# Attention in one kernel with an MLP: the output row tile of the preceding chunk in place of one step's weighted sums

## The chip, the cores and the metric

The kernel runs on one core of a Trainium2 chip. The metric is the device time of one execution in microseconds (us). Five engines work from queues of their own, each in program order: PE (TensorE: matmuls; its weight loads are shown as PEld), ACT (ScalarE), DVE (VectorE), POOL (GpSimd) and SP (SyncE, which here only issues DMAs). They wait for one another through semaphores.

## The reference

All of it is float32; x is 1 x 2048 x 448, there are 16 heads of 28 columns, and k and v have one head that all 16 query heads share.

```python
xn = _layernorm(x)
q = (xn @ wq).reshape(B, S, H, Dh).transpose(0, 2, 1, 3)     # H = 16, Dh = 28
k, v = xn @ wk, xn @ wv
p = softmax(einsum("bhqd,bkd->bhqk", q, k) * Dh ** -0.5)
o = einsum("bhqk,bkd->bhqd", p, v)                           # weighted sums
A = o.transpose(0, 2, 1, 3).reshape(B, S, H * Dh) @ wo       # output projection
y = _layernorm(xn)
Bm = gelu(y @ w1 + b1) @ w2 + b2                             # F = 1792
out = x + A + Bm
```

## The kernel before

The program has three stages: normalisation and the q, k, v projections; the MLP, whose result plus x is kept in DRAM (`ad`); and attention, which ends with the output projection. The instructions of each engine stand in the order in which the Python code emits them (a manual schedule), so the order of the loops is the order on every queue.

Attention works on 16 *units* `u`, numbered from 0. A unit is a chunk `c = u // 4` of 512 query rows and a group `g = u % 4` of four heads. A unit goes through 16 key tiles `kt` of 128 keys, in eight *steps* `i` = 0 to 7; `n = 8u + i` counts steps over all units. In each step the string ORDER says in which order kinds of work are emitted:

- `s`: a score, L694: one matmul of 128 keys by 512 queries for one head `j` into a PSUM tile `m`, and its exponential on ACT into a tile `p` (L695). SHARES gives eight or seven of these per step. `p` tiles come in 12 pairs (PAIRS), 24 in all.
- `M` and `X`, `Y`: preparation for the following units. `M` is a matmul for the score maxima (L523), whose transpose and reduce run on DVE (L530, L531); there is one in each of steps 3 to 6, in which only seven scores are done. `X` and `Y` shift, exponentiate (L538 on ACT) and transpose back (L544) the scores of the next unit's first key tile.
- `n`: one stage of the normalisation of the preceding unit's sums (L807 to L822), which ends in the pair `oth`, `otl` (the high and low part of the normalised sums, pool tiles with 5 buffers each, kept in `ots[c, g]`).
- `P`: the weighted sums, L880. BURST = 2 key tiles are taken from the queue `pvq`, each with four matmuls of 128 x 32 weights that write four bands of one PSUM tile `po`. In the trace each of them has two records. The queue runs behind the scores: step i of a unit sums key tiles 2i-2 and 2i-1, step 0 the last two of the unit before.
- `o`: one stage of the stream `oside`. When a chunk's fourth unit is summed, `o_wait` first loads four row tiles from `ad` over eight steps, and then `o_jobs` emits one *output row tile* per step through `o_part`: 12 matmuls of 128 x 128 weights and 448 columns (three for each of the four groups, L767 to L769) into one PSUM tile `m`, an add on DVE (L772) and a store (L773). The four row tiles of chunk 0 so fall into unit 5, those of chunk 1 into unit 9, those of chunk 2 into unit 13, in steps 1 to 4, between that step's scores. The row tiles of chunk 3 are done after the last unit (`end_jobs`), except a first part in the last step.

PSUM tiles `m` come from seven buffers in turn (`mtile`: four in `rings`, three in `mp`), for scores, maxima and row tiles alike: a matmul that starts a tile waits until the seventh tile before it has been read.

`load_rows_of` takes a tile `a` (four buffers), writes one element of it on DVE (L755) so that the load has something to wait on, and loads the row tile on SP's queue (L756).

Of the kernel before, what the change touches and what calls it, by code (L numbers as in the profile page):

```python
# [9 lines left out]
F32R = mybir.dt.float32r  # L10
# [5 lines left out]
P = 128  # L16
S, D, H, DH, F = 2048, 448, 16, 28, 1792
NT = S // P
CT = 4
NCH = NT // CT  # L20
CW = CT * P
NG = H // 4
# [3 lines left out]
BURST = 2  # L26
# [14 lines left out]
def block_kernel(ctx, tc, x, wq, wk, wv, wo, w1, b1, w2, b2, out):  # L41
# [4 lines left out]
    def f(t):  # L46
        return t.bitcast(F32)
# [62 lines left out]
    def mtile(shape):  # L110
        if rings:
            given.append(0)
            if len(given) % 7 > 3 or len(given) % 7 == 0:
                return rings[0].tile(shape, F32, name="m")
        return mp.tile(shape, F32, name="m")
# [94 lines left out]
    def bn_end(c, k0=0, n=CT):  # L210
        for k in range(k0, k0 + n):
            dve.bn_aggr(lnp[:, CT * c + k, :], sts[c][:, k, :])
        ts = slice(CT * c + k0, CT * c + k0 + n)
        r = rstd(lnr[:, ts], lnp[:, ts, 1], n)
        next(r)
        yield
        next(r)
        dve.scalar_tensor_tensor(lnb[:, ts], lnp[:, ts, 0], -1.0, lnr[:, ts], op0=ALU.mult, op1=ALU.mult)
        yield
# [9 lines left out]
    def norm_both():  # L229
        dve.tensor_mul(lnq, lnp[:, :, 1], lnr)  # L230
        dve.tensor_mul(lnq, lnq, lnr)
        r = rstd(lnq, lnq, NT)
        next(r)
        yield
        next(r)
        yield
        turned = mtile([NT, P])
        pe.transpose(turned, lnq, ident)
        rows = wp.tile([NT, P], F32, name="rows")
        dve.tensor_copy(rows, turned)  # L240
        nc.scalar.dma_start(second, rows)
        act.activation(warm, one, AF.Tanh)
        yield
# [162 lines left out]
    for c, at in ((2, ((0, 1), (0, 2), (0, 2), (0, 3))), (3, ((1, 0), (1, 1), (1, 2), (1, 3)))):  # L406
        for k in range(CT):
            later(*at[k], lambda t=CT * c + k: bn(t))
        g = bn_end(c)
        for k in range(2):  # L410
            later(c - 1, 0, lambda g=g: next(g), True)
    g = norm_both()
# [11 lines left out]
    units = [(c, g) for c in range(NCH) for g in range(NG)]  # L424
    NU = len(units)
    qss, ots = {}, {}
# [3 lines left out]
    for c in range(NCH):  # L430
        if c + 1 < NCH:
            center, turn = norm_parts(c + 1)
        for i in range(4):
# [17 lines left out]
            if (c, i) in w1_turns:  # L451
                n = w1_turns.index((c, i))
# [117 lines left out]
                    self.gens.pop(0)  # L570
            return False

    side, oside = Stream(), Stream()

    ph1b = ExitStack()
    hp = ph1b.enter_context(tc.tile_pool(name="hp", bufs=1))
# [124 lines left out]
    for n in range(len(mslots) + LAG):  # L701
        c, ft = mslots[n] if n < len(mslots) else (NCH, n - len(mslots))
# [29 lines left out]
    att = ctx.enter_context(tc.tile_pool(name="att", bufs=2))  # L732
# [19 lines left out]
    def load_rows_of(c, tiles):  # L752
        for k in tiles:
            rows[c, k] = keep.tile([P, D], F32, name="a", bufs=4)
            dve.memset(rows[c, k][0:1, 0:1], 0.0)  # L755
            nc.sync.dma_start(rows[c, k], ad[:, CT * c + k, :])  # L756
# [3 lines left out]
    def o_part(c, k, gs):  # L760
        if gs[0] == 0:
            parts[c, k] = mtile([P, D])
        po = parts[c, k]
        ts = slice(k * P, (k + 1) * P)
        for g in gs:
            oth, otl = ots[c, g]
            pe.matmul(po, oth[:, ts], woh[:, g, :], start=(g == 0), stop=False)  # L767
            pe.matmul(po, oth[:, ts], wol[:, g, :], start=False, stop=False)  # L768
            pe.matmul(po, otl[:, ts], woh[:, g, :], start=False, stop=(g == NG - 1))  # L769
        if gs[-1] == NG - 1:  # L770
            a = rows[c, k]
            dve.tensor_add(a, a, parts.pop((c, k)))  # L772
            (nc.scalar if k % 2 and c == NCH - 1 else nc.sync).dma_start(ov[:, CT * c + k, :], a)  # L773

    def o_jobs(c):
        for k in range(CT):
            o_part(c, k, range(NG))
            yield

    def o_tiles(c, g):  # L780
        ots[c, g] = [att.tile([P, CW], F32R, name=n, bufs=5) for n in ("oth", "otl")]
        return ots[c, g]

    def watch(u, sums):
# [5 lines left out]
    def judge_sum():  # L790
        whole = att.tile([P, 1], F32, name="whole", bufs=1)
        dve.tensor_reduce(whole, seen, axis=AX.X, op=ALU.add)
        return whole
# [29 lines left out]
        yield  # L823

    def end_jobs(u, po, halves_of):
        while side.step() or oside.step():
            pass
        c, g = units[u]
        oth, otl = o_tiles(c, g)
        tr, rb, on = att.tile([P, CW], F32, name="tr2", bufs=1), att.tile([P, CW], F32, name="tr", bufs=1), att.tile([P, CW], F32, name="oc", bufs=1)  # L830
        rc = att.tile([P, CW // 32], F32, name="rc", bufs=1)
        halves_of(1)
        sq = att.tile([P, CW], F32, name="sq", bufs=1)
        act.activation(sq, po, AF.Square, accum_out=seen[:, u:u + 1])
        for k in (1, 2):
            o_part(c, k, range(NG - 1))

        def blocks(t, h):
            return t[:, h].rearrange("p (a b) -> p a b", b=32)

        def shares(i):
            h, r = slice(256 * i, 256 * i + 256), slice(8 * i, 8 * i + 8)
            dve.transpose(tr[:, h], po[:, h])
            dve.reciprocal(rc[:, r], blocks(tr, h)[:, :, 0])
            dve.transpose(blocks(rb, h), rc[:, r, None].to_broadcast([P, 8, 32]))
            dve.tensor_mul(on[:, h], po[:, h], rb[:, h])
            act.activation(oth[:, h], on[:, h], AF.Copy)
            return lambda: dve.tensor_sub(otl[:, h], on[:, h], f(oth[:, h]))

        shares(0)()  # L850
        whole = judge_sum()
        low = shares(1)
        o_part(c, 0, [g])
        o_part(c, 1, [g])
        low()
        o_part(c, 3, range(NG - 1))
        judge(whole)
        o_part(c, 2, [g])
        o_part(c, 3, [g])
# [15 lines left out]
    def pv(u, kt):  # L875
        if kt == 0:
            pos[u] = op.tile([P, CW], F32, name="po")
        po = pos[u]
        for j in range(4):
            pe.matmul(po[32 * j:32 * j + 32, :], vs[:, kt, :], ps.pop((u, kt, j)),  # L880
                      start=(kt == 0), stop=(kt == NT - 1))
        if kt == NT - 1:
            side.add(norm_jobs(u, pos.pop(u)))
            side.step()
            c, g = units[u]
            if c < NCH - 1 and g == NG - 1:
                oside.add(o_wait(c))

    def o_wait(c):
        for k in range(CT):  # L890
            load_rows_of(c, [k])
            yield
            yield
        yield from o_jobs(c)

    xside = Stream()
    pvq = [(u, kt) for u in range(NU) for kt in range(NT)]
    last = NU * NT // 2 - 1
    for u in range(NU):
        todo = [(u, kt, j) for kt in range(1 if u else 2, NT) for j in range(4)]  # L900
        for i in range(NT // 2):
            n = NT // 2 * u + i
            if n == last - 13:
                load_rows_of(NCH - 1, range(CT))
            if n == 9:
                load_wo()
            if 12 <= n < 12 + NG:
                prep_wo(n - 12)
            if i == 0 and u + 2 < NU:
                load_q(u + 2)  # L910
            jobs = todo[:SHARES[i] if u else 8 * (i > 0)]
            todo = todo[len(jobs):]
            maxima = [(u + 2, i - 3 - (u == 0))] if 3 + (u == 0) <= i < 7 + (u == 0) else []
            if u == 0 and i in (1, 2):
                maxima = [(1, 2 * i - 2), (1, 2 * i - 1)]
            for what in ORDER:
                if what == "s" and jobs:
                    score(*jobs.pop(0))
                elif what == "M":
                    for v, j in maxima:  # L920
                        if v < NU:
                            max_job(v, j)
                elif what in "XY":
                    if what == "X" and i == (2 if u else 3) and u + 1 < NU:
                        xside.add(shift_jobs(u + 1))
                    xside.step()
                elif what == "e":
                    if i == 7 and u + 2 < NU:
                        load_max(u + 2)
                    if n == 2:  # L930
                        load_max(1)
                elif what == "n":
                    side.step()
                elif what == "o":
                    if n == last:
                        o_part(NCH - 1, 0, range(NG - 1))
                    oside.step()
                elif what == "P":
                    assert not jobs
                    for _ in range(BURST if n else 0):  # L940
                        pv(*pvq.pop(0))
        assert not todo
    assert pvq and all(u == NU - 1 for u, kt in pvq)
    pv_last(NU - 1, [kt for u, kt in pvq])
    while side.step():
        pass
    while oside.step():
        pass

    def full_max(u):  # L950
# [79 lines left out]
```

## Time and profile before

| | |
|---|---|
| median of 3 runs | 897.25 us (896.04 to 898.35) |
| the profiled execution | 897.27 us |
| its span, first to last instruction | 895.2 us |
| mean granted TensorE clock | 0.998 |

The attention stage fills a little more than the second half of the span: the first copy of L807, which ends unit 0, starts at 382.4 us, and the last one at 851.3 us. The profile's numbers are us from the start of the span, unless marked ns. In the rows of a timeline the first number is the start, the second how long the group of merged instructions lasted, and what stands in square brackets is the engine's idle time ahead of the group and what ended it.

### The profile page before, as it was taken

To read this page: it belongs to the slowest core of one execution; us is meant where nothing else is said; L and a number is where in the kernel's file an instruction comes from. 1 tells how busy PE (TensorE), PEld (TensorE's weight loads), DVE (VectorE), ACT (ScalarE), POOL (GpSimd) and SP (SyncE) were. 2 spreads that over 40 slices of the span, in tenths; PEclk is the share of its full clock that TensorE was granted. 3 is DMA by queue.
4 is the path that set the end of the run, shared out by engine and by line. 5 is a ranking of instruction groups with operands and counts; after the bars stand their busy time and mean duration, and the time that the engine had idled before them with its cause. 6 is when DMAs were issued, how large, how long until landed. Compare 5 with 4: busy or idle time off the path is not lost.

```text
span 895.2 us, 13235 instructions
## 1 busy us (share of the span) xinstructions
PE 883.6 (99%) x4914; PEld 563.6 (63%) x4914; DVE 485.4 (54%) x963; ACT 703.7 (79%) x1334; POOL 72.8 (8%) x82
## 2 busy tenths in 40 slices
PE   9999999999999999999999999999999999999997
PEld 8777888888888886444444564444564444564445
DVE  6757766656556767555464544464544564544212
ACT  5767564545454467999999979999969999969993
POOL 5450000000000002040000000000000000000000
PEclk9999999999999999999999999999999999999999
DMA  9975232023003004031102201102211102211001
GB/s 303 316 233 191 82 127 83 1 77 112 1 3 111 2 11 124 2 78 43 43 1 63 74 31 43 34 10 63 63 42 43 32 12 63 64 41 43 1 1 44
DMA packets 36297, 60.69 MB, mean 68 GB/s; under 512 B 7782, under 2 KB 23348, under 8 KB 35204
## 3 DMA queue, kind: packets, MB, share of 16 engines
q1 hardware_dynamic: 34644, 58.95, 21.7%
q10 hardware_dynamic: 1584, 0.84, 0.4%
q8 instruction: 40, 0.66, 0.3%
q14 instruction: 29, 0.24, 0.1%
HBM read 39.89 MB, written 18.88 MB: 66 GB/s over the span
## 4 chain that ended last, share of the span: by engine, by line
PE 86%; ACT 5%; DVE 4%; DMA 3%; issue 1%; SPq 0%; POOL 0%; ACTq 0%; DVEq 0%; POOLq 0%
PE m L694 27%; PE po L880 25%; PE ph L178 11%; PE m L630 4%; PE m L633 4%; PE m L627 4%; ACT p L695 2%; PE m L523 2%; PE m L767 1%; PE m L768 1%; PE m L769 1%; PE ph L181 1%; PE ph L183 1%; DMA qd<-qe 1%; PE qp L178 1%
## 5 line engine op out<-in xcount | busy, mean ns | idle before, releaser
L695 ACT ACTIVATE p<-m 128x512 f32<-128x512 f32 x956 | 491.2, 771 | 29.8 <-PE m L694 29.4
L694 PE MATMUL m<-xh,ks 128*128 128x512 f32 x960 | 272.7, 410 | 0.7 <-DVE tt L530 0.3
L694 PEld LDWEIGHTS m<-xh,ks 128*128 128x128 f32 x960 | 174.3, 188 | 149.4 <-ACT p L695 76.3
L880 PE MATMUL po<-p,vs 128*32 128x512 f32 x2016 | 242.4, 598 | 0.0
L880 PEld LDWEIGHTS po<-p,vs 128*32 128x32 f32 x2016 | 52.6, 109 | 115.9 <-issue 115.9
L600 ACT ACTIVATE hz<-hx,b1s 128x512 f32<-128x512 f32 x56 | 40.6, 724 | 101.8 <-DVE hx L597 101.8
L530 DVE STREAM_TRANSPOSE tt<-m 128x512 f32<-128x512 f32 x60 | 43.0, 716 | 111.3 <-PE m L523 111.3
L633 PE MATMUL m<-w2h,hl 128*128 128x448 f32 x224 | 81.9, 366 | 0.1
L627 PE MATMUL m<-w2h,hh 128*128 128x448 f32 x224 | 81.9, 366 | 0.0
L630 PE MATMUL m<-w2l,hh 128*128 128x448 f32 x224 | 81.9, 365 | 0.0
L604 DVE SCALAR_TENSOR_TENSOR hz<-hz,hx 128x512 f32<-128x512 f32 x56 | 38.8, 692 | 52.0 <-ACT hx L601 52.0
L807 DVE COPY oc<-po 128x512 f32<-128x512 f32 x15 | 10.4, 692 | 103.2 <-PE po L880 103.2
L178 PE MATMUL ph<-xh,w1h 128*128 128x512 f32 x159 | 63.1, 397 | 2.0 <-DVE hx L597 2.0
L178 PE MATMUL ph<-xh,w1l 128*128 128x512 f32 x159 | 62.3, 392 | 0.0
L178 PE MATMUL ph<-xl,w1h 128*128 128x512 f32 x159 | 62.3, 392 | 0.0
L822 POOL TENSOR_TENSOR otl<-oc,oth 128x512 fp32r<-128x512 f32 x15 | 23.9, 1591 | 470.2 <-DVE oth L820 244.5
L597 DVE TENSOR_TENSOR hx<-ph,xn 128x512 f32<-128x512 f32 x53 | 36.4, 687 | 39.8 <-PE ph L183 39.6
L538 ACT ACTIVATE tt<-tt 128x512 f32<-128x512 f32 x60 | 51.4, 857 | 0.0
L544 DVE STREAM_TRANSPOSE p<-tt 128x512 f32<-128x512 f32 x60 | 42.1, 702 | 12.0 <-ACT tt L538 12.0
L627 PEld LDWEIGHTS m<-w2h,hh 128*128 128x128 f32 x224 | 42.1, 188 | 5.4 <-issue 0.4
L630 PEld LDWEIGHTS m<-w2l,hh 128*128 128x128 f32 x224 | 42.1, 188 | 4.5
L633 PEld LDWEIGHTS m<-w2h,hl 128*128 128x128 f32 x224 | 42.1, 188 | 4.1 <-DVE hl L615 0.7
(173 smaller groups left out, 1032.2 us busy)
## 6 DMA issues: line engine op xcount, KB each, us to landing
xh<-qd SPq DMA_DIRECT2D x64, 224.0 KB
qd<-qe SPq DMA_DIRECT2D x24, 256.0 KB
a<-in_A_x_dram SPq DMA_DIRECT2D x20, 224.0 KB
ad<-a SPq DMA_DIRECT2D x16, 224.0 KB
a<-ad SPq DMA_DIRECT2D x16, 224.0 KB
raw<-in_B_w_dram SPq DMA_DIRECT2D x7, 448.0 KB
out_dram<-a SPq DMA_DIRECT2D x14, 224.0 KB
xd<-xh SPq DMA_DIRECT2D x2, 1024.0 KB
```

Of the source, the lines that this page charges most:

```text
L178: pe.matmul(ps, w, v, start=(n == 0), stop=False)
L530: dve.transpose(tts[u, j], pm)
L538: act.activation(tts[u, j], tts[u, j], AF.Exp, scale=SCALE)
L544: dve.transpose(p0s[u][:, j], tts.pop((u, j)))
L600: act.activation(hz, hx, AF.Square, bias=b1s[:, ft:ft + 1], scale=GELU[0] ** 0.5)
L604: dve.scalar_tensor_tensor(hz, hz, 1.0, hx, op0=ALU.add, op1=ALU.mult)
L627: pe.matmul(m2[k], hh[:, ts], w2h, start=(ft == 0), stop=False)
L630: pe.matmul(m2[k], hh[:, ts], w2l, start=False, stop=False)
L633: pe.matmul(m2[k], hl[:, ts], w2h, start=False, stop=(ft == NF - 1))
L694: pe.matmul(s, ks[:, kt * P:(kt + 1) * P], qss[u][:, j, :], start=True, stop=True)
L695: act.activation(p, s, AF.Exp, scale=SCALE)
L880: pe.matmul(po[32 * j:32 * j + 32, :], vs[:, kt, :], ps.pop((u, kt, j)), start=(kt == 0), stop=(kt == NT - 1))
```

## The change

Row tiles of chunks 0 to 2 are no longer a stream of their own. Each unit from 4 on does one of them: unit u does row tile u % 4 of chunk u // 4 - 1, in step 5, at the place `P` where that step's two key tiles would be summed. These two are summed in step 6 with step 6's own, four key tiles in a row. The row tile's row is loaded at the start of the unit; the rows of the last chunk are loaded in the last two steps. `oth` and `otl` get 8 buffers each, since a chunk's pairs are now kept until the next chunk's last unit. `oside`, `o_wait` and its calls go.

```diff
     def o_tiles(c, g):
-        ots[c, g] = [att.tile([P, CW], F32R, name=n, bufs=5) for n in ("oth", "otl")]
+        ots[c, g] = [att.tile([P, CW], F32R, name=n, bufs=8) for n in ("oth", "otl")]
...
         if kt == NT - 1:
             side.add(norm_jobs(u, pos.pop(u)))
             side.step()
-            c, g = units[u]
-            if c < NCH - 1 and g == NG - 1:
-                oside.add(o_wait(c))
-
-    def o_wait(c):
-        for k in range(CT):
-            load_rows_of(c, [k])
-            yield
-            yield
-        yield from o_jobs(c)
...
+    o_steps = {(u, 5): (u // NG - 1, u % NG) for u in range(NG, NU)}
...
-            if n == last - 13:
-                load_rows_of(NCH - 1, range(CT))
+            if n >= last - 1:
+                load_rows_of(NCH - 1, (range(CT - 1), [CT - 1])[n - last + 1])
+            for v, step in o_steps:
+                if v == u and i == 0:
+                    load_rows_of(o_steps[v, step][0], [o_steps[v, step][1]])
...
                 elif what == "o":
                     if n == last:
                         o_part(NCH - 1, 0, range(NG - 1))
-                    oside.step()
                 elif what == "P":
                     assert not jobs
-                    for _ in range(BURST if n else 0):
+                    if (u, i) in o_steps:
+                        o_part(*o_steps[u, i], range(NG))
+                        continue
+                    for _ in range((BURST if n else 0) * (1 + ((u, i - 1) in o_steps))):
                         pv(*pvq.pop(0))
```

On PE before, in unit 5 at the end of step 1's row tile and the start of step 2 (`m` is a PSUM tile, `xh` the queries, `ks` the keys, `woh` the high part of wo, `vs` the values; the sum matmuls are counted without the trace's doubling):

```order
L769 MATMUL m<-woh,otl 128x448
L694 MATMUL m<-xh,ks 128x512 x3
L880 MATMUL po<-p_4712,vs 32x512 x4
L880 MATMUL po<-p,vs 32x512 x4
L694 MATMUL m<-xh,ks 128x512 x5
L767 MATMUL m<-woh,oth 128x448
L768 MATMUL m<-wol,oth 128x448
L769 MATMUL m<-woh,otl 128x448
```

A row tile stands between five scores and three, and the sums of two key tiles follow in every step.

On PE now, in unit 4 at the end of step 5's row tile, and on through step 6 into the following steps (`km` is the keys' sample for the maxima):

```order
L769 MATMUL m<-woh,otl 128x448
L694 MATMUL m<-xh,ks 128x512
L523 MATMUL m<-xh,km 128x512
L694 MATMUL m<-xh,ks 128x512 x6
L880 MATMUL po<-p,vs 32x512 x16
L694 MATMUL m<-xh,ks 128x512 x8
L880 MATMUL po<-p,vs 32x512 x8
```

Between step 5's scores and step 6's stands the row tile alone; the sums of step 5 have moved behind step 6's scores and make one run of 16 with those that stood there.

On DVE now, in unit 4, steps 5 and 6 (`tt` is the tile of the maxima and shifted scores, `mr` the maxima, `a` the output row):

```order
L530 STREAM_TRANSPOSE tt<-m 128x512
L531 TENSOR_REDUCE mr_4696<-tt 128x16
L544 STREAM_TRANSPOSE p_4712<-tt 128x512
L535 TENSOR_TENSOR tt<-tt,mq 128x512
L772 TENSOR_TENSOR a<-a,m 128x448
L530 STREAM_TRANSPOSE tt<-m 128x512
L531 TENSOR_REDUCE mr_4696<-tt 128x16
L544 STREAM_TRANSPOSE p_4712<-tt 128x512
```

The add of the row tile (L772) stands between the work of step 5 and the transpose of step 6; before, no add stood in this unit.

More of the change, by code (lines that the diff above doesn't have):

```diff
@@ L571, in step @@
             return False
-    side, oside = Stream(), Stream()
+    side = Stream()
     ph1b = ExitStack()
@@ L825, in end_jobs @@
     def end_jobs(u, po, halves_of):
-        while side.step() or oside.step():
+        while side.step():
             pass
@@ L945, in block_kernel @@
     while side.step():
-        pass
-    while oside.step():
         pass
```

## Prediction

> **What bounds the kernel now.** First the page: the span, and who is busy in it.
>
> ```profile
> span 895.2 us, 13235 instructions
> PE 883.6 (99%) x4914; PEld 563.6 (63%) x4914; DVE 485.4 (54%) x963; ACT 703.7 (79%) x1334; POOL 72.8 (8%) x82
> ```
>
> The change lies in the attention stage, from unit 4 on. The view by windows is read next, cut at the starts of the copies of L807 (one per unit): us of the stretch, then busy time of PE, PEld, DVE, ACT, POOL, clock, DMA share, GB/s.
>
> ```profile
> 508.50:549.50 41.00, 41.00 (x241) 23.76 (x241) 18.86 (x39) 32.39 (x65) 1.66 (x1) 1.00 0.16 43
> 549.50:581.00 31.50, 31.50 (x193) 14.68 (x193) 16.41 (x34) 31.50 (x66) 1.61 (x1) 1.00 0.12 25
> 820.30:851.30 31.00, 31.00 (x189) 13.90 (x189) 9.25 (x20) 31.00 (x65) 1.58 (x1) 1.00 0.10 31
> ```
>
> A unit without output row tiles takes 31.5, and both PE and ACT look full. A unit with four of them (48 more matmuls: 241 against 193) takes 41.0, and there ACT has idle time. So PE sets the end in those units; in the others PE and ACT are close. The starts of the copies and the ends of ACT's idle times make it sharper:
>
> ```profile
> L807 DVE COPY oc<-po x15: 690/692/693, 382.4 to 851.3; 128x512 f32<-128x512 f32 x15
> ...
> 508.50 0.69 DVE L807 COPY oc<-po 128x512 f32<-128x512 f32 x1 [6.91 <-PE po L880]
> 549.47 0.69 DVE L807 COPY oc<-po 128x512 f32<-128x512 f32 x1 [6.92 <-PE po L880]
> ...
> ACT p L695 <- PE m L694: 26.4, 29, 1.3
> 512.44 1.57 ACT L695 ACTIVATE p<-m 128x512 f32<-128x512 f32 x3 [1.02 <-PE m L694]
> 515.18 2.56 ACT L695 ACTIVATE p<-m 128x512 f32<-128x512 f32 x5 [1.17 <-PE m L694]
> ```
>
> The unit with row tiles lasts 549.47-508.50 = 40.97. There are three of these among the 14 intervals of the first row (382.4 to 851.3, 468.9 in all), and a last one of 31.0, so the other ten average (468.9-3x40.97-31.0)/10 = 31.50. A row tile thus costs (40.97-31.50)/4 = 2.37, and twelve cost 28.4. ACT waits for scores 26.4 in all, about 2.2 per row tile: it stands still while PE computes one.
>
> **What a step of PE is made of.** Eight score matmuls (L694), then the sums of two key tiles (L880, 16 records, four at a time):
>
> ```profile
> 541.45 2.14 PE L694 MATMUL m<-xh,ks 128*128 128x512 f32 x8
> 543.51 1.92 PE L880 MATMUL po<-p,vs 128*32 128x512 f32 x16
> 545.37 2.11 PE L694 MATMUL m<-xh,ks 128*128 128x512 f32 x8
> 547.40 1.92 PE L880 MATMUL po<-p,vs 128*32 128x512 f32 x16
> 549.26 2.14 PE L694 MATMUL m<-xh,ks 128*128 128x512 f32 x8
> ...
> 543.97 0.13 PEld L880 LDWEIGHTS po<-p,vs 128*32 128x32 f32 x4 [0.30 <-issue]
> 544.40 0.13 PEld L880 LDWEIGHTS po<-p,vs 128*32 128x32 f32 x4 [0.30 <-issue]
> ...
> 521.55 1.10 PE L694 MATMUL m<-xh,ks 128*128 128x512 f32 x4
> 534.21 1.56 PE L694 MATMUL m<-xh,ks 128*128 128x512 f32 x6
> ```
>
> A step is (549.26-541.45)/2 = 3.905. From its first score to its first sum it takes 2.06 or 2.03, mean 2.045; a score more within a run costs (1.56-1.10)/2 = 0.23, so eight are 1.84 and 0.2 is lost at the two ends of the run. The sums take 545.37-543.51 = 1.86; a group of four records follows the one before by 544.40-543.97 = 0.43, so four are 1.72 and 0.14 is lost. **One pass from scores to sums and back therefore costs about 0.35**, and this is what the change can save, once per unit.
>
> Steps that also hold a max matmul (L523) are a little longer (one score fewer, so the same eight matmuls):
>
> ```profile
> 557.07 0.50 PE L694 MATMUL m<-xh,ks 128*128 128x512 f32 x1
> 561.17 0.50 PE L694 MATMUL m<-xh,ks 128*128 128x512 f32 x1
> 565.11 0.50 PE L694 MATMUL m<-xh,ks 128*128 128x512 f32 x1
> ...
> 557.54 0.80 ACT L538 ACTIVATE tt<-tt 128x512 f32<-128x512 f32 x1
> 561.40 0.88 ACT L538 ACTIVATE tt<-tt 128x512 f32<-128x512 f32 x1
> 565.26 0.96 ACT L538 ACTIVATE tt<-tt 128x512 f32<-128x512 f32 x1
> ```
>
> The first takes 4.10 and the next 3.94, that is 0.19 and 0.03 over 3.905: ACT does the exponential of tt ahead of the scores', and the eighth PSUM tile waits for it. Four such steps give about 0.28 of PE waiting for ACT per unit. In the unit with row tiles this waiting is gone, which closes the account: 12 matmuls of a row tile run from 509.58 to 512.01,
>
> ```profile
> 509.58 0.37 PE L767 MATMUL m<-woh,oth 128*128 128x448 f32 x1
> ...
> 511.81 0.36 PE L769 MATMUL m<-woh,otl 128*128 128x448 f32 x1
> 512.01 0.85 PE L694 MATMUL m<-xh,ks 128*128 128x512 f32 x3
> 512.21 0.62 DVE L772 TENSOR_TENSOR a<-a,m 128x448 f32<-128x448 f32 x1 [0.62 <-PE m L769]
> ```
>
> which is 2.43; four are 9.72, and 9.72-0.28 = 9.44 against the 9.47 measured.
>
> **The change part by part.**
>
> 1. *Row tile in place of step 5's sums, four key tiles in step 6.* Per unit from 4 to 15: the same 12 row-tile matmuls (+2.43, as before; the row tile stands among 128*128 matmuls before and after, so its surroundings cost the same), the same sums, one pass fewer (-0.35). Of the 0.28 of waiting, steps 3 and 4 come ahead of the row tile and keep theirs; steps 5 and 6 lose about 0.05. A unit becomes 31.50+2.43-0.35-0.05 = 33.53, that is 2.03 per row tile. Bounds: if all 0.28 goes, 1.80; if nothing of the pass or the waiting is saved, 2.43.
>
> 2. *Units 4 to 13*: 10 x 2.03 = 20.3. *Unit 14* has no max matmul (seven PE matmuls in steps 3 to 6, eight for ACT), and PE waits for ACT there:
>
> ```profile
> 838.90 2.09 PE L694 MATMUL m<-xh,ks 128*128 128x512 f32 x7
> 842.77 2.65 PE L694 MATMUL m<-xh,ks 128*128 128x512 f32 x8
> 847.21 2.13 PE L694 MATMUL m<-xh,ks 128*128 128x512 f32 x8
> ...
> 858.96 1.88 PE L694 MATMUL m<-xh,ks 128*128 128x512 f32 x7
> 866.32 1.88 PE L694 MATMUL m<-xh,ks 128*128 128x512 f32 x7
> ```
>
> Its step 6 takes 3.87 where an unhindered step of seven takes (866.32-858.96)/2 = 3.68, and its step 7 takes 4.44 where 3.91 is the norm: 0.72 of waiting that falls behind the new row tile and is covered by it. The row tile costs 2.43-0.35-0.72 = 1.36. *Unit 15*, whose steps of 3.68 show no waiting: 2.43-0.35 = 2.08. Together 20.3+1.4+2.1 = 23.8 in place of 28.4: **4.6 us gained**.
>
> 3. *What runs while PE is away from the scores.* ACT starts a step's eight tiles 565.26-561.40 = 3.86 apart, and the durations of its tt rows grow by 0.08 a step, so it needs between 3.86 and 3.94 per step (0.48 to 0.49 a job), at most 31.5 per unit. During the row tile it has the tail of step 5: eight jobs from about 0.24 after the step's start (565.26 against 565.11 and before it 561.40 against 561.17), so until some 4.2 after it, about when the row tile ends (1.95+2.43 = 4.4). Behind step 6's scores it has some seven jobs, 3.4 us, and the next score comes after 8x0.43+0.14+0.5 = 4.1 (0.5 for the first score's duration): ACT idles around 1 to 2 us there. 31.5 plus that stays at or below 33.53, so PE remains the bound.
>
> 4. *The burst's inputs.* It reads key tiles 8 to 11; the last of these are step 5's exponentials, done by the end of the row tile. The 24 p tiles are exactly in use when step 6's exponentials are done, and each of those takes a tile freed by step 4's sums. Cost 0; cover gone, PE would wait in the burst.
>
> 5. *The PSUM tile of the row tile.* It is the seventh matmul after it that reuses it, and no sums lie between any more: it starts about 0.2+0.34+5x0.24 = 1.7 after the start of the row tile's last matmul. The add of L772 ends at 512.21+0.62-511.81 = 1.02 after that. Margin 0.7 with DVE free at that time, which the order gives: the add stands ahead of step 6's transpose, and step 5's DVE work ends about 3.4 after the step's start:
>
> ```profile
> 567.85 0.65 DVE L535 TENSOR_TENSOR tt<-tt,mq 128x512 f32<-128x512 f32 x1
> 569.81 0.72 DVE L530 STREAM_TRANSPOSE tt<-m 128x512 f32<-128x512 f32 x1 [1.31 <-PE m L523]
> 570.56 0.69 DVE L531 TENSOR_REDUCE mr<-tt 128x16 f32<-128x512 f32 x1
> ```
>
> (0.65 on from 567.85, against 565.11), a microsecond ahead of the row tile's end. The two rows under it are the transpose and reduce of a next step. Cost 0.
>
> 6. *Row loads, memsets, stores, oth/otl with 8 buffers.* One load and one 1x1 memset per unit stand at the unit's start, ahead of its loads of q on SP, and wait for a store of four units ago. The stores on SP follow the add and have nothing behind them until step 7. For the last chunk, three loads come in the last unit's step 6 and one in step 7, ahead of the last scores; that one's memset waits for the store of step 5's row tile, which was issued about 1 after the row tile's end, some 4 us (1.81+3.55 less 1) earlier; DVE has only the final work behind it, and the row is added some 12 us later. Cost 0; were the load late by d, the end would be late by d at most.
>
> **Sum.** The profiled execution took 897.27, 2.07 more than its span, and the median of the runs is 897.25, so the sum is made on 897.27: 897.27-4.6 = **892.7**. A measurement here can tell 0.3%, 2.7 us, from no change.
>
> **The rivals.**
>
> *No gain: ACT paces the steps* (chance 0.15). The windows show ACT busy for all of 31.50. If the 0.35 is PE waiting for exponentials rather than its own loss, one pass fewer saves nothing: 10x2.38+1.7+2.43 = 27.9 in place of 28.4, so 896.8. The Trainium skill, "TensorEngine Tiling (Array Packing)", "PSUM Bottleneck", speaks for it: column tiles speed up the matmuls, but not the emptying of PSUM, which may become the bottleneck. Against it: in the last unit, steps with seven exponentials last 3.68, so 0.23 goes with one matmul while ACT would give back 0.48 with one exponential (3.86/8); and steps without a max matmul hold 3.905 in a row though ACT could do 3.86.
>
> *More gain: the row tile's slack absorbs all waiting for ACT* (0.10). Then 10x1.80+1.4+2.1 = 21.5, gained 6.9, so 890.4. For it: in the unit with row tiles the waiting vanishes. Against: there the row tiles stand in steps 1 to 4, ahead of or in the steps that wait; now the row tile is in step 5, and five steps lie between it and the next unit's step 3.
>
> *Slower: the row tile's PSUM tile comes free late* (0.10). If the add of L772 gets behind other DVE work, step 6's seventh matmul waits. Behind one transpose and reduce (0.72 and 0.69, which start after the max matmul, so the add would end at about 3.0 instead of 1.02), PE waits 1.3 per unit, 12x1.3 = 15.6, so 908. It turns the sign once the add is later by 0.7+4.6/12 = 1.1. Against: the order on DVE and the free microsecond ahead.
>
> *The change doesn't do what it says*: the order shows the bursts of 16, so it does; less than 0.03, with any other mishap.
>
> **How the numbers follow.** The forecast's own range, 1.80 to 2.2 per row tile, is 890.5 to 894.5, with 0.62. With the stronger gain (0.10) and some half of the no-gain rival (up to 896.8) the range 890.3 to 896.8 leaves out less than 0.2. Faster by over 0.3% (below 894.6): 0.72. Within 0.3%: 0.18. Slower: 0.10.
>
> **What the profile after would show.** Units 4 to 13 all about 33.5 long, unit 14 some 32.4; the row tile's 12 matmuls still 2.43; the burst of 32 records 3.55 to the next score; the first max step still 4.1; ACT's idle time once per unit, between 1 and 2 us, in the burst and not in the row tile. Wrong would be: a first sum of the burst that waits for ACT, a seventh score in step 6 that waits for DVE, units of 33.8 or more.

## The result, and the profile after

| | before | after |
|---|---|---|
| median of 6 runs each | 897.61 us (896.04 to 899.46) | 893.27 us (891.71 to 893.42) |
| the profiled execution | 897.27 us | 891.71 us |
| its span | 895.2 us | 889.8 us |

The ratio of after to before is 0.9946, with a 95% interval of 0.9931 to 0.9960: 3.6 to 6.2 us less. The forecast was 892.7, that is 4.6 less than the profiled execution of before.

The page of after has the same engines busy as before, and DVE and ACT nearly as long:

```profile
span 889.8 us, 13236 instructions
PE 878.8 (99%) x4914; PEld 565.4 (64%) x4914; DVE 485.7 (55%) x963; ACT 701.9 (79%) x1334; POOL 73.2 (8%) x82
```

The two profiled executions differ by 5.4 in span, but not all of that is the change's. The first copy of L807, which ends unit 0 and lies ahead of everything that was changed, comes 1.0 earlier in the execution after, and what follows the last matmul (the last add and store) is 0.4 shorter. Between those two points, which this document calls *the stage*, before takes 507.23 and after 503.15: **4.08 less**. The copies show how it is spread:

```profile
L807 DVE COPY oc<-po x15: 691/692/693, 381.4 to 844.2; 128x512 f32<-128x512 f32 x15
...
515.00:548.50 33.50, 33.50 (x206) 17.08 (x204) 17.03 (x36) 31.55 (x65) 1.67 (x2) 1.00 0.16 42
ACT p L695 <- PE m L694: 24.0, 14, 2.0
```

The ten intervals with the row tiles of units 4 to 13 lie between 33.49 and 33.59 (mean 33.52), where before had 31.5 with 41.0 among them. Over one such unit the view by windows (same columns as before) shows ACT busy for 31.55 of 33.50. In the view of the waits ACT's time without scores has fallen only from 26.4 to 24.0, but it now comes in 14 pieces of up to 2.0 instead of 29.

Unit 5's steps 3 to 7 on PE (timeline; start, duration, and the merged instructions):

```profile
517.16 0.50 PE L694 MATMUL m<-xh,ks 128*128 128x512 f32 x1
...
521.20 0.50 PE L694 MATMUL m<-xh,ks 128*128 128x512 f32 x1
...
525.13 0.50 PE L694 MATMUL m<-xh,ks 128*128 128x512 f32 x1
...
527.13 0.37 PE L767 MATMUL m<-woh,oth 128*128 128x448 f32 x1
...
529.56 0.39 PE L694 MATMUL m<-xh,ks 128*128 128x512 f32 x1
529.78 0.39 PE L523 MATMUL m<-xh,km 128*128 128x512 f32 x1
530.01 1.52 PE L694 MATMUL m<-xh,ks 128*128 128x512 f32 x6
531.46 3.64 PE L880 MATMUL po<-p,vs 128*32 128x512 f32 x32
535.03 2.10 PE L694 MATMUL m<-xh,ks 128*128 128x512 f32 x8
```

Steps 3 and 4 take 4.04 and 3.93, close to the 4.10 and 3.94 of before; the row tile takes 529.56-527.13 = 2.43; the scores behind it start without the 0.1 that they lose behind sums (0.22 from the first one to the next matmul, where it is 0.34 in step 5, behind sums); the burst follows at once and gives way to the next score after 3.57 (535.03-531.46). ACT and DVE beside it:

```profile
529.21 0.98 ACT L538 ACTIVATE tt<-tt 128x512 f32<-128x512 f32 x1
529.98 3.63 ACT L695 ACTIVATE p<-m 128x512 f32<-128x512 f32 x7
535.57 15.79 ACT L695 ACTIVATE p<-m 128x512 f32<-128x512 f32 x32 [1.95 <-PE m L694]
...
529.76 0.62 DVE L772 TENSOR_TENSOR a<-a,m 128x448 f32<-128x448 f32 x1 [1.22 <-PE m L769]
530.29 0.71 DVE L530 STREAM_TRANSPOSE tt<-m 128x512 f32<-128x512 f32 x1
```

ACT works through the row tile and stands still once, for 1.95, in the burst. The add ends at 530.38, and the seventh tile after the row tile's starts at about 530.92 (530.01 + 4x0.227), 0.54 later. In the trace it is this seventh tile whose weight load waits on DVE's semaphore, in each of units 4 to 15.

### The profile page after: what moved, and what is told of

Same layout as the page of the kernel before. It is cut to its first block, busy times and chain, and to the rows that moved or that the text cites. A ratio compares the mean times of both kernels' runs of the same rounds, so it can differ in the third digit from the quotient of the medians.

```text
span 889.8 us, 13236 instructions
## 1 busy us (share of the span) xinstructions
PE 878.8 (99%) x4914; PEld 565.4 (64%) x4914; DVE 485.7 (55%) x963; ACT 701.9 (79%) x1334; POOL 73.2 (8%) x82
## 4 chain that ended last, share of the span: by engine, by line
PE 83%; ACT 8%; DVE 4%; DMA 2%; issue 1%; SPq 0%; ACTq 0%; DVEq 0%
PE m L694 25%; PE po L880 24%; PE ph L178 11%; ACT p L695 5%; PE m L627 4%; PE m L633 4%; PE m L630 4%; PE m L767 2%; PE m L523 2%; PE m L769 1%; PE m L768 1%; PE ph L181 1%; PE ph L183 1%; PE qp L178 1%; DMA raw<-in_B_w_dram 1%
## 5 line engine op out<-in xcount | busy, mean ns | idle before, releaser
L694 PE MATMUL m<-xh,ks 128*128 128x512 f32 x960 | 268.8, 409 | 0.7 <-DVE tt L530 0.3
L880 PE MATMUL po<-p,vs 128*32 128x512 f32 x2016 | 239.9, 598 | 0.0
L807 DVE COPY oc<-po 128x512 f32<-128x512 f32 x15 | 10.4, 692 | 120.3 <-PE po L880 120.3
L538 ACT ACTIVATE tt<-tt 128x512 f32<-128x512 f32 x60 | 53.4, 890 | 0.0
L607 ACT ACTIVATE hz<-hz 128x512 f32<-128x512 f32 x56 | 35.2, 629 | 12.0 <-DVE hz L604 12.0
```

The lines of the kernel that those rows point to most:

```text
L538: act.activation(tts[u, j], tts[u, j], AF.Exp, scale=SCALE)
L694: pe.matmul(s, ks[:, kt * P:(kt + 1) * P], qss[u][:, j, :], start=True, stop=True)
```

## The experiments

The time of a whole run of the same code varied by up to 4.1 us (891.78 to 895.92 in one kernel), and the profiles show where: the first copy came between 380.9 and 384.4, and the end 5.1 to 6.8 after the last matmul, in stretches that no experiment's edit touched. The stage repeated well (503.15 in both profiles of the changed kernel). So the experiments are compared by the stage and by its units, and the times are given beside: one run each, or the median of six.

| kernel | stage | units 4 to 13, mean interval | unit 14 | time of the run |
|---|---|---|---|---|
| before | 507.23 | 31.5, and 41.0 in three | 31.08 | 897.27 |
| after | 503.15 | 33.52 | 33.09 | 891.71 |
| row tile per unit, sums not merged | 507.99 | 33.92 | 33.46 | 896.62 |
| before, with sums merged | 518.35 | 32.2 to 33.2, and 41.5 to 42.3 | 32.18 | 908.97 |
| one more pass per unit | 507.05 | 33.84 | 33.37 | 898.23 |
| add 1.2 later | 509.77 | 34.09 | 33.91 | 900.99 |
| row tile amid step 3 | 502.80 | 33.30 in six, 33.93 in four | 32.37 | median 892.6 |
| row tile amid step 5 | 504.05 | 33.5 in seven, 34.09 in three | 32.37 | median 893.14 |
| after, again | 503.15 | 33.52 | 33.09 | median 892.9 |
| row tile at the end of step 3 | 502.49 | 33.51 | 32.57 | median 892.3 |
| small matmul in step 7: fp32r, 128 columns of weights | 504.50 | 33.63 | 33.12 | 894.68 |
| the same: fp32, 128 columns | 505.71 | 33.73 | 33.27 | 895.07 |
| the same: fp32, 32 columns | 509.79 | 34.08 | 33.57 | 900.27 |
| the same: fp32r, 32 columns | 504.57 | 33.63 | 33.16 | 894.3 |

### One part alone: the row tiles spread, the sums not merged

```diff
                     if (u, i) in o_steps:
                         o_part(*o_steps[u, i], range(NG))
-                        continue
-                    for _ in range((BURST if n else 0) * (1 + ((u, i - 1) in o_steps))):
+                    for _ in range(BURST if n else 0):
```

> The row tile stays one per unit in step 5, but each step keeps its own two key tiles (the row tile is followed by step 5's sums). Theory: the pass from scores to sums and back costs PE about 0.35 and is what was saved, so units 4 to 13 go from 33.5 to 33.86 and the whole is 4.2 above the changed kernel, where the kernel before was. Rival (ACT paces the steps; spreading the row tiles is what helped): units stay at 33.5 and the time at the changed kernel's.

The stage took 507.99, 0.8 more than before and 4.8 more than after; the units 33.92, 0.40 more than after. In the timeline of this kernel, step 6's first score behind sums, and step 6's own sums:

```profile
530.15 1.92 PE L880 MATMUL po<-p,vs 128*32 128x512 f32 x16
532.00 0.50 PE L694 MATMUL m<-xh,ks 128*128 128x512 f32 x1
...
534.04 1.92 PE L880 MATMUL po<-p,vs 128*32 128x512 f32 x16
535.89 2.14 PE L694 MATMUL m<-xh,ks 128*128 128x512 f32 x8
```

Step 6 takes 534.04-532.00 = 2.04 from its first score to its first sum and 535.89-534.04 = 1.85 for its sums. That is what a step took in the kernel before, so the pass is back with both its losses.

Spreading the row tiles over the units gains nothing by itself (it costs 0.8). In this layout the whole gain is in the pass that the merging takes away.

### The other part alone: the sums merged, the row tiles left where they were

The kernel before, with one edit:

```diff
-                    for _ in range(BURST if n else 0):
+                    for _ in range((BURST if n else 0) * ((1, 1, 1, 1, 1, 0, 2, 1)[i] if u >= NG else 1)):
                         pv(*pvq.pop(0))
```

> The kernel before with its row tiles where they were; only the sums of step 5 move into step 6 in units 4 to 15. Theory: without a row tile between them, 16 scores in a row fill the seven PSUM tiles and wait for ACT, and ACT then runs dry in the burst of four key tiles (3.57 and the first score against 7 jobs of 0.48): units without row tiles grow from 31.5 by 0.5 to 1.0 although PE has one pass less; the whole is 4 to 9 above the kernel before. Rival (a pass less is worth 0.35 wherever it goes): each unit 0.35 shorter, the whole 4.2 below.

The stage grew by 11.1: the direction is as expected, the size beyond the expected 4 to 9: units without row tiles grew by 0.7 to 1.7 (32.2 to 33.2) and not by 0.5 to 1.0. In a unit without row tiles (steps 5 to 7, PE and ACT):

```profile
566.03 0.50 PE L694 MATMUL m<-xh,ks 128*128 128x512 f32 x1
...
571.62 0.50 PE L694 MATMUL m<-xh,ks 128*128 128x512 f32 x1 [0.50 <-ACT p L695]
572.05 3.64 PE L880 MATMUL po<-p,vs 128*32 128x512 f32 x32
575.62 2.14 PE L694 MATMUL m<-xh,ks 128*128 128x512 f32 x8
576.23 15.79 ACT L695 ACTIVATE p<-m 128x512 f32<-128x512 f32 x32 [1.72 <-PE m L694]
```

The 16 score and max matmuls take from 566.03 to 572.05, 6.02 in place of some 4.1 (twice 2.045), because PE waits for the exponentials to free PSUM tiles; then ACT has nothing for 1.72. So a pass less was worth nothing here, where nothing filled PE's time between the two runs of scores. In the changed kernel the row tile does that: it needs PE for 2.43 and no exponentials. The two parts lose 0.8 and 11.1 alone and gain 4.1 together.

### One pass more

The changed kernel, with one of step 7's two key tiles summed between the fourth and the fifth score in units 4 to 15:

```diff
-            for what in ORDER:
+            for at, what in enumerate(ORDER):
+                if at == 9 and i == 7 and u >= NG:
+                    pv(*pvq.pop(0))
...
-                    for _ in range((BURST if n else 0) * (1 + ((u, i - 1) in o_steps))):
+                    for _ in range((BURST if n else 0) * (1 + ((u, i - 1) in o_steps)) - (i == 7 and u >= NG)):
```

> The changed kernel with one more pass in step 7 of units 4 to 15: one of its two key tiles is summed after the fourth score, the other at the end. Theory: +0.35 per unit (33.5 to 33.85), +4.2 in all, and the interrupted run of scores shows the lost time at its ends. Rival (ACT paces): no change, ACT has idle time ahead of step 7 anyway.

Units 33.84, 0.32 more, and the stage 3.9 more: taking a pass away and putting one in give nearly the same size, 0.40 and 0.32 around the 0.35 of the prediction. The interrupted run of scores, and ACT beside it:

```profile
536.93 1.20 PE L694 MATMUL m<-xh,ks 128*128 128x512 f32 x4
538.06 1.06 PE L880 MATMUL po<-p,vs 128*32 128x512 f32 x8
539.05 1.21 PE L694 MATMUL m<-xh,ks 128*128 128x512 f32 x4
...
537.47 16.12 ACT L695 ACTIVATE p<-m 128x512 f32<-128x512 f32 x32 [1.97 <-PE m L694]
```

Four scores at 0.23 are 0.92 of the 1.13 up to the first sum, and two groups of sums at 0.43 are 0.86 of the 0.99 behind it, so 0.21 and 0.13 are lost at the two ends. ACT did not set this: it had idled 1.97 in the burst just before, and its 32 exponentials now take 16.12, where they took 15.79 in the changed kernel, so it gives way to PE. The run's time of 898.23 is 6.5 above that of after; 1.5 of this lies ahead of the stage and 1.1 behind its last matmul.

### The row tile's PSUM tile set free later

The changed kernel with two more reads of each row tile's PSUM tile ahead of the add:

```diff
+            if c < NCH - 1:
+                for _ in range(2):
+                    dve.tensor_copy(att.tile([P, CW], F32, name="sq", bufs=1)[:, 0:D], po)
             dve.tensor_add(a, a, parts.pop((c, k)))
```

> The changed kernel with two more DVE reads of each row tile's PSUM tile (chunks 0 to 2) ahead of the add, about 0.62 each, so that the tile comes free 1.24 later. In the changed kernel's trace the add ends at 530.38 and the seventh matmul after the row tile starts at 530.92, a margin of 0.5. Theory: PE waits 0.7 per unit in step 6, units 33.5 to 34.2, +8 in all, the place and price of the rival that would have made it slower. If the margin is covered otherwise (ACT behind, or PE ahead): no change.

Here the copies are L774 and the add is L775:

```profile
531.01 1.28 DVE L774 COPY sq<-m 128x448 f32<-128x448 f32 x2 [1.24 <-PE m L769]
531.28 1.32 PE L694 MATMUL m<-xh,ks 128*128 128x512 f32 x5
532.21 0.61 DVE L775 TENSOR_TENSOR a<-a,m 128x448 f32<-128x448 f32 x1
...
532.88 0.50 PE L694 MATMUL m<-xh,ks 128*128 128x512 f32 x1 [0.28 <-DVE a L775]
```

The units grow by 0.57 on average (expected 0.7), the stage by 6.6, and the view of the waits (390 to 850) names the add:

```profile
PE m L694 <- DVE a L775: 2.9, 8, 0.5
```

But it is not always the seventh tile that waits. In the unit shown, the seventh starts at 532.20 (the last of the five), the add ends at 532.82, and it is the eighth that waits, until 532.88. So it is in six of units 4 to 13, which take 34.07 to 34.15. In unit 7 the seventh waits for the add (34.39), and in unit 9 the seventh waits too, though the profile puts that wait down to ACT (34.47). In units 4 and 11 neither waits for it, and they take 33.74 and 33.68, still about 0.2 more than in the changed kernel; the cause of that 0.2 stays open. The buffers of the PSUM tiles thus do not turn strictly in sevens, as the description of the kernel has it; what decides their turn, no run here shows. So the rival that would have made the change slower exists and costs about what was argued, and the changed kernel, where the seventh tile is the one concerned, has 0.54 to spare.

### The waits that are left: the row tile in three other places

These aim at a version better than both. Two put the row tile behind the fifth score of its step, one in step 3 (with the burst in step 4) and one in step 5; the third puts it behind the last score of step 3. With the row tile in step 3, 26 p tiles are live. The edit for step 3 follows; the kernel with step 5 leaves out its first two pairs of lines.

```diff
-PAIRS = 12
+PAIRS = 13
...
-    o_steps = {(u, 5): (u // NG - 1, u % NG) for u in range(NG, NU)}
+    o_steps = {(u, 3): (u // NG - 1, u % NG) for u in range(NG, NU)}
...
                 elif what == "o":
                     if n == last:
                         o_part(NCH - 1, 0, range(NG - 1))
+                    if (u, i) in o_steps:
+                        o_part(*o_steps[u, i], range(NG))
                 elif what == "P":
                     assert not jobs
                     if (u, i) in o_steps:
-                        o_part(*o_steps[u, i], range(NG))
                         continue
```

> The changed kernel with the row tile in step 3 after its fifth score (not behind the last one), the four key tiles in step 4, and 13 pairs of p tiles, since 26 tiles are live there. The waits of PE for ACT begin in step 3. Theory: the row tile gives ACT the time to catch up ahead of them, so about 0.25 per unit goes: units 4 to 13 33.27, unit 14 32.4 (its 0.69 ahead of the row tile goes too); 3.2 below the changed kernel. Rival (ACT's own work of 31.5 plus its 2.0 of idle time in the burst already fill the unit): units stay at 33.5.

> The changed kernel with the row tile in step 5 after its fifth score instead of behind the last one, sums as in the changed kernel. Theory: in unit 14, without a max matmul, the row tile's PSUM tile is the eighth of the step and waits for ACT; ahead of the last scores it is not, so unit 14 goes from 33.09 to 32.4, the others lose at most 0.05; 0.7 to 1.2 below the changed kernel. Rival (the wait in unit 14 is ACT's backlog and comes back at the next score): unit 14 stays at 33.1.

> The changed kernel once more, as the measure for the other two on the same chip: ratio to before 0.995, units 33.5.

Unit 14 went to 32.37 in both, as expected: its wait was at the row tile. The rest of both expectations failed. Of the other units six took 33.30 in the first kernel, as expected, but four took 33.93 (in the second, 33.5 in seven and 34.09 in three, where at most 0.05 more was expected). The stage was 0.35 shorter than the changed kernel's in the first, where 3.2 was expected, and 0.9 longer in the second, where 0.7 to 1.2 less was. The timelines of a long and a short unit of the first kernel part at the eighth tile of step 4:

```profile
491.53 1.30 PE L694 MATMUL m<-xh,ks 128*128 128x512 f32 x5
493.18 0.50 PE L694 MATMUL m<-xh,ks 128*128 128x512 f32 x1 [0.35 <-ACT p L695]
493.61 3.64 PE L880 MATMUL po<-p,vs 128*32 128x512 f32 x32
...
525.46 1.53 PE L694 MATMUL m<-xh,ks 128*128 128x512 f32 x6
526.92 3.64 PE L880 MATMUL po<-p,vs 128*32 128x512 f32 x32
```

In the trace the weight load of this matmul waits on ACT's semaphore in units 4, 6, 11 and 13, the four long ones, and on DVE's in the other six. In the second kernel the eighth tile of step 6 waits on ACT's in units 5, 10 and 12, again the long ones, and on DVE's in the other seven. By the count of tiles, ACT's stands for the buffer of the step's first score, seven tiles back, and DVE's for that of the max matmul, six tiles back: here too the buffers do not turn strictly in sevens. ACT comes late to that first score, since the two scores behind the row tile are ahead of it. The ratios to before were 0.9954 (0.9940 to 0.9967) and 0.9960 (0.9948 to 0.9972), beside 0.9960 (0.9946 to 0.9974) for the changed kernel in the same comparison, so neither can be told from it by the times.

The third kernel differs from the changed one by the lines of PAIRS and `o_steps` alone.

> The changed kernel with the row tile behind the last score of step 3 (not step 5), the four key tiles in step 4, 13 pairs of p tiles. In the run with the row tile after the fifth score of step 3, six of ten units took the 33.3 that was expected and four took 33.9: there the eighth tile of step 4 waits for the exponential of that step's first score, which ACT reaches late, since two scores, not done before the row tile, stand ahead of it. Theory: with all scores ahead of the row tile that wait is gone, and the waits of steps 4 to 6 too; the wait inside step 3 stays in part. All ten units at 33.3 to 33.4, unit 14 below 33.0, 1.5 to 2.7 below the changed kernel. Rival (ACT's work and its idle time fill the unit): 33.5.

The long units are gone, and unit 14 took 32.57, but the ten units stayed at 33.51. The expectation of 33.3 failed: step 3 takes 2.15 up to the row tile,

```profile
484.20 0.50 PE L694 MATMUL m<-xh,ks 128*128 128x512 f32 x1
...
486.35 0.36 PE L767 MATMUL m<-woh,oth 128*128 128x448 f32 x1
```

against 2.00 in step 5 of the changed kernel (527.13-525.13). The wait of 0.15 in the first max step is thus paid whole, and it is as much as steps 3 and 4 of the changed kernel lose together (0.13 and 0.03 over 3.905). What this kernel gains, 0.66 in the stage, is mostly unit 14's (0.52). Its ratio to before, 0.9938 (0.9923 to 0.9953), can't be told from the changed kernel's.

### What in a pass costs

Four kernels put one small matmul (128 columns of keys) behind the fourth score of step 7 of units 4 to 15, in four forms.

```diff
+                if at == 9 and i == 7 and u >= NG:
+                    pe.matmul(mtile([P, P])[0:32, :], ks[:, 0:32], ks[:, 0:P], start=True, stop=True)
```

This is the last of the four; the others take `ks[:, 0:P]` in fp32r, the same in fp32, and `vs[:, 0, :]` in fp32 as weights, and the rows of the result to match; the two fp32 ones read the keys as fp32 too. Each takes one PSUM tile out of the turn, which nothing reads.

> What the pass costs, 1 of 4: the changed kernel with one small matmul (128 columns of keys) after the fourth score of step 7 in units 4 to 15, in the scores' own form: fp32r, 128x128 weights. No change of form: units 4 to 13 grow by its own 0.07 or so and no more.

> What the pass costs, 2 of 4: the same small matmul in fp32 with 128x128 weights. If the pass costs because of the type (fp32r to fp32 and back), units grow by the small matmul's own fp32 time plus up to 0.3; if because of the tile form, by its own time alone.

> What the pass costs, 3 of 4: the same small matmul in the sums' form, fp32 with 128x32 weights. Both explanations: its own time plus about 0.3.

> What the pass costs, 4 of 4: the same small matmul in fp32r with 128x32 weights. If the tile form is what costs, its own time plus about 0.3; if the type, its own time alone (about 0.07).

Against the changed kernel the units grew by 0.12 (fp32r, 128 columns of weights), 0.21 (fp32, 128), **0.56** (fp32, 32) and 0.12 (fp32r, 32). The timelines of the second, the third and the fourth:

```profile
535.22 1.20 PE L694 MATMUL m<-xh,ks 128*128 128x512 f32 x4
536.25 0.38 PE L912 MATMUL m<-ks 128*128 128x128 f32 x2
536.39 1.17 PE L694 MATMUL m<-xh,ks 128*128 128x512 f32 x4
...
536.13 1.20 PE L694 MATMUL m<-xh,ks 128*128 128x512 f32 x4
537.25 0.41 PE L912 MATMUL m<-ks,vs 128*32 128x128 f32 x2
537.59 1.21 PE L694 MATMUL m<-xh,ks 128*128 128x512 f32 x4
...
535.18 1.20 PE L694 MATMUL m<-xh,ks 128*128 128x512 f32 x4
536.21 0.22 PE L912 MATMUL m<-ks 128*32 128x128 f32 x1
536.27 1.15 PE L694 MATMUL m<-xh,ks 128*128 128x512 f32 x4
```

Only the sums' own form opens gaps on both sides: 1.12 from the first of four scores to it, where the other two come after 1.03, and 0.34 to the next score where the fp32 one with 128 columns needs 0.14 and the fp32r one 0.06. Against the fp32 matmul with 128 columns, which has the same two records, the 32 columns cost 0.35 more per unit, which is the size of a pass. So it is not the type alone, and the count of columns alone does not do it either; the two together do. (The fp32 weights of 32 columns are those of `vs`, all the others those of `ks`; that the tile makes no difference was not tested.) Whether the fp32r matmul with 32 columns used the array in another way than the fp32 one, the records don't show.

## Why the prediction was right, and where it was off

**What bounds the stage**: right. PE sets the length of the units with row tiles in both kernels: ACT was busy for 32.39 of 41.00 before and is for 31.55 of 33.50 now, and the stage's length follows from PE's own account.

**A pass costs 0.35**: right. A unit was to take 33.53 and takes 33.52. The rival that ACT paces the steps would have left the merging without effect; unmerged sums cost 0.40 per unit and one more pass 0.32, and in the kernel with one more pass ACT was idle just ahead and then slower for it. Why a pass costs this, beyond the form of the sums' matmuls, stays open.

**Units 4 to 13**: forecast 20.3 for their row tiles, measured 335.2-10x31.5 = 20.2 (335.2 is the sum of the ten intervals). The waits of steps 3 and 4 stayed, as forecast, so the rival of more gain did not come.

**Unit 14**: this term was mis-sized, 1.36 forecast and 33.09-31.08 = 2.01 measured (so the unit's 32.4 became 33.09). The prediction had the 0.72 of waiting fall behind the row tile and be covered. Instead PE waits ahead of it:

```profile
826.11 1.89 PE L694 MATMUL m<-xh,ks 128*128 128x512 f32 x7
828.44 0.47 PE L767 MATMUL m<-woh,oth 128*128 128x448 f32 x1 [0.44 <-ACT p L695]
```

The row tile starts 2.33 after its step's first score; seven scores of the last unit, whose row tile does not wait, take 1.71:

```profile
859.21 1.88 PE L694 MATMUL m<-xh,ks 128*128 128x512 f32 x7
860.92 0.37 PE L767 MATMUL m<-woh,oth 128*128 128x448 f32 x1
```

In units 4 to 13 the row tile waits on DVE's semaphore: seven tiles back is the step's max matmul, which DVE reads early. Units 14 and 15 have no max matmul, and there it waits on ACT's, for the step's first score; in unit 14 ACT has not done that exponential yet. The runs with the row tile amid the scores took the wait away (32.37, which is 1.29 over 31.08 and near the 1.36 of the forecast). This confirms the place.

**Unit 15**: 2.08 forecast, 40.27-38.25 = 2.02 measured, from the last copy to the last matmul.

**The sum** for the stage is therefore 4.1 where 4.6 was forecast, nearly all of the difference in unit 14. That the median fell by 4.3 and the profiled execution by 5.6 has to do with the stretches around the stage, which vary by more than that difference.

**ACT in the burst**: right: idle once per unit, 1.95, and not during the row tile; the burst never waited for its inputs. **The add's margin**: 0.7 forecast, 0.54 measured; nothing waited, and the run with a later add shows that PE would have, at the seventh tile or at the eighth. **Loads and memsets**: the last memset (L755) did wait 2.3 on DVE for a store, with nothing behind it, as the prediction allowed:

```profile
DVE a L755 <- DMA out_dram<-a: 2.3, 1, 2.3
```

## What to carry to other kernels

In this kernel a change of form on PE had a price that could be read ahead as the difference between the matmuls' spacing within a run and the distance across its ends, and longer runs saved it. But longer runs only paid where ACT, which empties the scores' PSUM tiles, had a stock of work for their length: the merging alone lost 11.1, and gained only with other PE work put where the scores would have waited. And the waits that such a step adds or removes depend on which earlier tile its PSUM buffer held. So count the tiles back to it for each unit that is built differently, and check in a trace whose semaphore the matmul waits on, since in three kernels here the count of seven did not hold throughout.

## What was not expected of the hardware

A single matmul of 128x32 fp32 weights between scores cost 0.35 more than one of 128x128 fp32 weights, while in fp32r 32 columns and 128 columns both cost 0.12. And equal code repeated to within 0.01 in the stage (two profiles of the changed kernel) but varied by 3.5 ahead of it (first copy at 380.9 to 384.4) and by 1.7 behind its last matmul, so that a gain of half a per cent was seen far better in the units than in the times. Ahead of the stage the longest of these profiles, with 384.4, shows a granted clock of 0.97 between 40 and 100 us, where the other profiles show 1.00; what makes the others differ by up to 2.0 stays open.
